# Storing the last output tile in halves of 64 rows, and a last piece of 160 columns

## The chip, the cores and the metric

The kernel runs on one core of a Trainium2 chip. The metric is the device time of one execution in microseconds. The profile is of one execution, and its span (from the first to the last instruction) is some 1.8 us shorter than the time of the same execution (393.5 against 395.35 us before the change).

## The reference

```python
# attention: q, k, v are (8, 12, 448, 64)
scores = scale * (q @ k^T) - log(448)
attn   = sigmoid(scores)
x      = (attn @ v)  -> (8*448, 768)
# feed-forward part: w_in (768, 2048), w_out (2048, 768)
h   = x @ w_in
g   = gelu_tanh(h)
out = g @ w_out      # (3584, 768), float32
```

## The kernel before

The kernel is a static schedule: a planner orders all operations, then they are written out per engine. Only its end matters here. The output is made in 28 tiles of 128 rows x 768 columns. The 128 rows of a tile are two strips of 64 rows each, and the 64 rows of a strip lie 7 rows apart in the output (row `r*7 + j` belongs to strip `j`). A tile is computed in column pieces; each piece is 16 matmuls into one PSUM bank (where TensorE leaves its sums), an eviction (the copy from there into the on-chip buffer `ob` in SBUF), and stores (transfers from `ob` to `out` in DRAM). A store is issued by an engine's instruction (about 0.5 us in this trace) and carried out by DMA engines, of which the profile counts 16 for the core; it has landed when the semaphore that it raises shows it done. SyncE (SP) issues the stores, except the very last half, which ScalarE (ACT) issues.

```python
def pieces(t_):
    if t_ < NT - 1:
        return [(0, EH), (EH, DM)]                           # 384 + 384 columns
    return [(0, EH), (EH, DM - 128), (DM - 128, DM)]         # last tile: 384, 256, 128

def make_b(t_, x, t):
    ...                                                      # 16 matmuls, eviction `ev` into ob[o]
    last = t_ == NT - 1
    end = last and hi == DM                                  # the last piece of the last tile
    ...
    if hi == DM or last:
        left = lo if last else 0
        if last and not end:                                 # pieces 0 and 1 of the last tile
            b, j = two[0]
            dst = out[b*S:(b+1)*S, lo:hi].rearrange("(r j) d -> j r d", j=NJ)[j:j + 2]
            # one transfer: DRAM side 2 x 64 x (hi-lo), SBUF side 128 x (hi-lo)
            sts.append(plan.add(Op("st%d" % t_, "SP", lambda e: e.dma_start(dst, ob[o][:, lo:hi]), ...)))
            return op
        for y in range(2):                                   # everything else: two transfers of 64 rows
            b, j = two[y]
            dst = out[b*S:(b+1)*S, left:hi].rearrange("(r j) d -> r j d", j=NJ)[:, j, :]
            def fn(e, y=y, dst=dst):
                return e.dma_start(dst, ob[o][64*y:64*y + 64, left:hi])
            if end and y == 1:
                at_end.append((fn, ev))                      # ACT issues it, after its last eviction
                continue
            sts.append(plan.add(Op("st%d.%d" % (t_, y), "SP", fn, ...)))
    ...
# at the end SP waits for the semaphores of the last three tiles' stores, then for ACT's store
```

Of the kernel before, what the change touches and what calls it, by code (L numbers as in the profile page):

```python
# [279 lines left out]
def bass_sigmoid_attention__then__act_gelu_tanh_kernel(  # L280
# [8 lines left out]
    B, H, S, D = q.shape  # L289
    assert D == 64 and H % 4 == 0 and S % 64 == 0 and B % 2 == 0  # L290
    NJ = S // 64
    NG = H // 4
    DM, DF = moe_w_in.shape
# [3 lines left out]
    EH = DM // 2  # L297
# [24 lines left out]
    plan = Plan()  # L322

    with contextlib.ExitStack() as stack:
        def SB(name, shape, dt):
            return stack.enter_context(nc.sbuf_tensor(name, shape, dt))
# [19 lines left out]
        ob = [SB("ob%d" % i, [128, DM], F32) for i in range(NOUT)]  # L346
# [4 lines left out]
        def copy(e, o, i, who):  # L351
            if who == "ACT":
                return e.activation(o, i, AF.Copy)  # L353
            return e.tensor_copy(o, i)  # L354

        def copy_alts(n):
            return {"ACT": (n / 1.2 + 50, n / 1.2 + 190), "DVE": (n / 0.96 + 75, n / 0.96 + 150)}
# [4 lines left out]
            out=ident[:], in_=ident[:], compare_op=ALU.not_equal, fill=1.0, base=0,  # L362
# [15 lines left out]
        def take(t):  # L378
            ok = [i for i in range(NPS) if bank_ok(i, t)]
            lone = [i for i in ok if not bank_ok(i ^ 1, t)]  # L380
            i = (lone or ok)[0]
            bank_busy[i] = True
            return i
# [12 lines left out]
        def give(i, op):  # L396
            bank_free[i] = op
            bank_busy[i] = False
# [363 lines left out]
        def pieces(t_):  # L762

            if t_ < NT - 1:
                return [(0, EH), (EH, DM)]
            return [(0, EH), (EH, DM - 128), (DM - 128, DM)]

        def make_b(t_, x, t):
            bank = take(t)
            prev = bank_free[bank]  # L770
            two = strips[2 * t_:2 * t_ + 2]
            col = (2 * t_ * 64) % (2 * S)
            lo, hi = pieces(t_)[x]

            def fn(e):
                r = None
                for fc in range(FC):
                    r = mm(ps[:, bank, 0:hi - lo], gT[:, fc, col:col + 128], w_out[:, fc, lo:hi],  # L778
                           start=(fc == 0), stop=(fc == FC - 1))
                return r  # L780

            deps = [prev] + [gelu[(b, fc)] for b in {x[0] for x in two} for fc in range(FC)]
            if t_ < 8:
                for ops in w_out_ld.values():
                    deps += ops
            op = Op("b%d.%d" % (t_, x), "PE", fn, deps, FC * ((hi - lo) / 2.4 + 2.5), 165.0, mode=128)
            o = t_ % NOUT
            edeps = [op]
            if t_ >= NOUT:
                edeps += store[t_ - NOUT]  # L790
            last = t_ == NT - 1
            end = last and hi == DM
            alts = copy_alts(hi - lo)
            if end:
                del alts["DVE"]
            ev = plan.add(Op("evo%d.%d" % (t_, x), "ANY",
                             lambda e, who: copy(e, ob[o][:, lo:hi], ps[:, bank, 0:hi - lo], who),
                             edeps, 0, 0, prio=(0, -1), alts=alts))
            give(bank, ev)
            ev_o[(t_, x)] = ev  # L800
            for (b, j) in two:
                if j == NJ - 1 or (b == B - 1):
                    b_last[b] = op
            if hi == DM or last:
                sts = store.setdefault(t_, [])
                left = lo if last else 0
                if last and not end:
                    b, j = two[0]
                    dst = out[b * S:(b + 1) * S, lo:hi].rearrange("(r j) d -> j r d", j=NJ)[j:j + 2]
                    sts.append(plan.add(Op("st%d" % t_, "SP", lambda e: e.dma_start(dst, ob[o][:, lo:hi]), [ev], 500.0, 0.0,  # L810
                                           prio=(0, t_), sem="st%d.0.%d" % (o, x), pkt=(8, 145.0))))
                    return op
                for y in range(2):
                    b, j = two[y]
                    dst = out[b * S:(b + 1) * S, left:hi].rearrange("(r j) d -> r j d", j=NJ)[:, j, :]

                    def fn(e, y=y, dst=dst):
                        return e.dma_start(dst, ob[o][64 * y:64 * y + 64, left:hi])

                    if end and y == 1:  # L820
                        at_end.append((fn, ev))
                        continue
                    sts.append(plan.add(Op("st%d.%d" % (t_, y), "SP", fn,
                                           [ev] if last else [ev_o[(t_, 0)], ev_o[(t_, 1)]], 500.0, 0.0,
                                           prio=(0, t_), sem="st%d.%d.%d" % (o, y, x if last else 0), pkt=(4, 145.0))))
            return op
# [103 lines left out]
        def pe_next(pl, t):  # L930
# [58 lines left out]
            if go_a:  # L989
                b, fc = state["a"]  # L990
                op = make_a(b, fc, t)
                state["a"] = (b, fc + 1) if fc + 1 < FC else (b + 1, 0)
                return op
            op = make_b(state["b"], state["h"], t)
            if state["h"] == len(pieces(state["b"])) - 1:
                for (b, j) in strips[2 * state["b"]:2 * state["b"] + 2]:
                    if j == NJ - 1:
                        b_done.add(b)
                state["b"] += 1
                state["h"] = 0  # L1000
            else:
                state["h"] += 1
# [21 lines left out]
        sem = {nm: stack.enter_context(nc.semaphore("s_" + nm.replace(".", "_"))) for nm in names}  # L1024
# [71 lines left out]
```

## Time and profile before

| | before |
|---|---|
| time, median of 3 runs | 395.26 us |
| span of the profiled execution | 393.5 us |
| TensorE busy | 381.8 us, 97% |
| last matmul ends | 385.58 us |
| last eviction ends | 385.88 us |
| tail: span minus end of the last matmul | 7.9 us |

The page of the profile says at its top that TensorE (PE) is busy nearly all the time (PEld are its weight loads, DVE is VectorE, POOL is GpSimd):

```profile
span 393.5 us, 7448 instructions
...
PE 381.8 (97%) x3189; PEld 201.2 (51%) x3189; DVE 134.4 (34%) x230; ACT 241.0 (61%) x380; POOL 51.1 (13%) x82
```

One would stop there, but a share is an average over the span. The chain of waits, asked for the time from 380 us on, ends with the last eviction. Its columns are start and duration in us:

```profile
379.84 5.74 PE ps L778 x51
385.58 0.02 issue
385.60 0.28 ACT ob L353
```

The chain stops at 385.88 us and the span is 393.5 us. The 7.6 us that are missing are no instruction of a compute engine, so the chain does not show them. The timeline of the same stretch shows what is issued there (start, us, engine, line, operation):

```profile
382.96 0.49 ACT L353 ACTIVATE ob<-ps 128x384 f32<-128x384 f32 x1 [2.11 <-PE ps L778]
383.48 2.18 SPq L810 DMA_DIRECT2D out_dram<-ob  x2
384.71 0.38 ACT L353 ACTIVATE ob<-ps 128x256 f32<-128x256 f32 x1 [1.26 <-PE ps L778]
385.60 0.28 ACT L353 ACTIVATE ob<-ps 128x128 f32<-128x128 f32 x1 [0.51 <-PE ps L778]
385.91 0.50 SPq L818 DMA_DIRECT2D out_dram<-ob  x1
385.91 0.54 ACTq L818 DMA_DIRECT2D out_dram<-ob  x1
```

Three evictions, and the stores after each: two single transfers of 128 rows (line 810, starting at 383.48 and 385.1 us) and the last piece's two halves (line 818). The DMA view, from 383.3 us on, gives size and time from issue to landing:

```profile
out_dram<-ob SPq DMA_DIRECT2D x1, 192.0 KB
out_dram<-ob SPq DMA_DIRECT2D x1, 128.0 KB
out_dram<-ob SPq DMA_DIRECT2D x1, 32.0 KB, 7.1
out_dram<-ob ACTq DMA_DIRECT2D x1, 32.0 KB, 4.4
```

For the two transfers of 128 rows the profile has no landing time. The last and smallest ones, 32 KB each, took 7.1 and 4.4 us, while a store of 192 KB with 64 rows takes 2.7 us (median) in the tiles before. What the DMA engines did meanwhile is in the table by windows; its last two columns are the mean busy share of the 16 DMA engines and the rate:

```profile
core 0: us, PE busy (x) PEld busy (x) DVE busy (x) ACT busy (x) POOL busy (x), PEclk, DMA share, GB/s
385.00:386.00 1.00, 0.57 (x11) 0.39 (x7) 0.00 (x0) 0.37 (x2) 0.00 (x0) 1.00 0.16 38
386.00:387.00 1.00, 0.00 (x0) 0.00 (x0) 0.00 (x0) 0.00 (x0) 0.00 (x0) 1.00 0.12 26
387.00:388.00 1.00, 0.00 (x0) 0.00 (x0) 0.00 (x0) 0.00 (x0) 0.00 (x0) 1.00 0.26 51
388.00:389.00 1.00, 0.00 (x0) 0.00 (x0) 0.00 (x0) 0.00 (x0) 0.00 (x0) 1.00 0.42 98
389.00:390.00 1.00, 0.00 (x0) 0.00 (x0) 0.00 (x0) 0.00 (x0) 0.00 (x0) 0.53 0.14 49
390.00:391.00 1.00, 0.00 (x0) 0.00 (x0) 0.00 (x0) 0.00 (x0) 0.00 (x0) 0.50 0.14 48
391.00:392.00 1.00, 0.00 (x0) 0.00 (x0) 0.00 (x0) 0.00 (x0) 0.00 (x0) 0.50 0.14 48
392.00:393.00 1.00, 0.00 (x0) 0.00 (x0) 0.00 (x0) 0.00 (x0) 0.00 (x0) 0.50 0.08 26
```

Nothing but DMA runs after 386 us. Its share is 0.12 to 0.14 in four of the seven windows from there on: two of sixteen engines are a share of 0.125. It is higher from 387 to 389 us (0.26 and 0.42), where most rows of the last piece's two small stores are moved as well.

### The profile page before, as it was taken

To read this page: it belongs to the slowest core of one execution; us is meant where nothing else is said; L and a number is where in the kernel's file an instruction comes from. 1 tells how busy PE (TensorE), PEld (TensorE's weight loads), DVE (VectorE), ACT (ScalarE), POOL (GpSimd) and SP (SyncE) were. 2 spreads that over 40 slices of the span, in tenths; PEclk is the share of its full clock that TensorE was granted. 3 is DMA by queue.
4 is the path that set the end of the run, shared out by engine and by line. 5 is a ranking of instruction groups with operands and counts; after the bars stand their busy time and mean duration, and the time that the engine had idled before them with its cause. 6 is when DMAs were issued, how large, how long until landed. Compare 5 with 4: busy or idle time off the path is not lost.

```text
span 393.5 us, 7448 instructions
## 1 busy us (share of the span) xinstructions
PE 381.8 (97%) x3189; PEld 201.2 (51%) x3189; DVE 134.4 (34%) x230; ACT 241.0 (61%) x380; POOL 51.1 (13%) x82
## 2 busy tenths in 40 slices
PE   7899999999999999999999999999999999999991
PEld 5344455545544554545555545555555555555561
DVE  3356613146435562464524434244332200000000
ACT  5999953588669877685757575756666533333110
POOL 5992110011102101110111010110000000000000
PEclk9999999999999999999999999999999999999997
DMA  8999999576774996595665918855030103011331
GB/s 232 199 198 203 210 207 310 112 176 151 173 178 127 215 169 170 83 261 122 172 166 96 184 36 188 163 117 151 2 80 3 32 10 82 0 40 42 80 82 40
DMA packets 64149, 51.74 MB, mean 131 GB/s; under 512 B 36212, under 2 KB 60660, under 8 KB 64116
## 3 DMA queue, kind: packets, MB, share of 16 engines
q1 hardware_dynamic: 48820, 36.78, 38.5%
q0 software_dynamic: 14528, 13.64, 21.9%
q10 hardware_dynamic: 768, 0.85, 0.6%
q8 instruction: 25, 0.41, 0.4%
q14 instruction: 8, 0.07, 0.1%
HBM read 45.61 MB, written 11.01 MB: 144 GB/s over the span
## 4 chain that ended last, share of the span: by engine, by line
PE 94%; ACT 3%; POOL 0%; issue 0%; POOLq 0%
PE ps L778 37%; PE ps L733 37%; PE ps L598 9%; PE ps L646 7%; ACT at L609 3%; PE ps L407 1%; PE ps L709 1%; PE ps L555 1%; PE ps L552 0%; POOL ident L361 0%; ACT ob L353 0%; POOL ident L360 0%; POOLq L361 0%; POOLq L1081 0%
## 5 line engine op out<-in xcount | busy, mean ns | idle before, releaser
L778 PE MATMUL ps<-w_out,gT 128*128 128x384 bf16 (+2 forms) x912 | 152.8, 323 | 0.0
L733 PE MATMUL ps<-xT,w_in 128*128 128x448 bf16 x750 | 151.7, 353 | 0.0
L622 DVE TENSOR_SCALAR at<-th 128x896 bf16<-128x896 f32 x147 | 91.8, 629 | 134.9 <-ACT th L618 134.8
L618 ACT ACTIVATE th<-ps 128x896 f32<-128x896 f32 x147 | 130.0, 931 | 0.5 <-PE ps L598 0.5
L778 PEld LDWEIGHTS ps<-w_out,gT 128*128 128x128 bf16 x912 | 87.6, 98 | 61.8 <-issue 3.6
L733 PEld LDWEIGHTS ps<-xT,w_in 128*128 128x128 bf16 x750 | 70.2, 98 | 74.0 <-issue 6.1
L747 ACT ACTIVATE gT<-ps 128x448 bf16<-128x448 f32 x128 | 71.3, 559 | 40.7 <-PE ps L733 40.7
L353 ACT ACTIVATE ob<-ps 128x384 f32<-128x384 f32 (+2 forms) x57 | 27.7, 485 | 96.7 <-PE ps L778 96.7
L598 PE MATMUL ps<-qT,kT 64*64 64x448 bf16 x672 | 49.1, 359 | 2.2 <-ACT at L609 1.7
L484 POOL DMA_DIRECT2D vb<-in_v_dram x24 | 15.0, 624 | 209.5 <-PE ps L598 206.2
L646 PE MATMUL ps<-at,vb 64*64 64x448 bf16 x672 | 38.2, 350 | 0.0
L598 PEld LDWEIGHTS ps<-qT,kT 64*64 64x64 bf16 x672 | 15.1, 105 | 28.2 <-issue 15.9
L646 PEld LDWEIGHTS ps<-at,vb 64*64 64x64 bf16 x672 | 19.5, 107 | 12.0 <-issue 0.7
L354 DVE CAST xT<-ps 128x448 bf16<-128x448 f32 x27 | 16.5, 619 | 11.9 <-PE ps L646 11.8
L354 DVE CAST kb<-kf 128x896 bf16<-128x896 f32 (+2 forms) x21 | 12.6, 601 | 18.5 <-DMA kf<-in_k_dram 18.4
L609 ACT ACTIVATE at<-ps 128x896 bf16<-128x896 f32 x21 | 17.1, 953 | 0.7 <-PE ps L598 0.7
L486 POOL DMA_DIRECT2D vb<-in_v_dram x24 | 17.4, 724 | 0.2 <-issue 0.2
L354 DVE CAST qb<-qf 128x896 bf16<-128x896 f32 (+1 forms) x20 | 12.2, 610 | 8.6 <-DMA qf<-in_q_dram 8.6
L353 ACT ACTIVATE xT<-ps 128x448 bf16<-128x448 f32 x21 | 11.8, 561 | 2.2 <-PE ps L646 2.2
L839 POOL DMA_DIRECT2D w_in<-in_moe_w_in_dram x16 | 9.9, 659 | 0.0
L407 PE MATMUL ps<-gT,ident 128*128 128x256 bf16 x25 | 5.6, 387 | 1.5 <-POOL ident L361 1.5
L354 DVE COPY kT<-ps 128x896 bf16<-128x896 bf16 (+2 forms) x7 | 3.9, 553 | 3.3 <-PE ps L552 1.7
(29 smaller groups left out, 39.9 us busy)
## 6 DMA issues: line engine op xcount, KB each, us to landing
out_dram<-ob SPq DMA_DIRECT2D x55, 192.0 KB, 2.8
kf<-in_k_dram SPq DMA_DIRECT2D x19, 448.0 KB, 4.5
qf<-in_q_dram SPq DMA_DIRECT2D x18, 448.0 KB, 6.1
vb<-in_v_dram POOLq DMA_DIRECT2D x48, 112.0 KB, 5.4
w_in<-in_moe_w_in_dram POOLq DMA_DIRECT2D x16, 192.0 KB, 10.7
w_out<-in_moe_w_out_dram POOLq DMA_DIRECT2D x4, 768.0 KB, 22.0
kb<-in_k_dram POOLq DMA_DIRECT2D x4, 224.0 KB, 8.5
qb<-in_q_dram POOLq DMA_DIRECT2D x4, 224.0 KB, 8.7
```

Source lines behind the costliest of these rows:

```text
L353: return e.activation(o, i, AF.Copy)
L354: return e.tensor_copy(o, i)
L484: a = plan.add(Op("ldv%da" % g, "SWQ", lambda e, d=dst[0:64], ap=lo: e.dma_start(d, ap), deps, 610.0, 0.0, prio=order_v(g), sem="ldv%da" % ...
L486: c = plan.add(Op("ldv%db" % g, "SWQ", lambda e, d=dst[64:128], ap=hi: e.dma_start(d, ap), deps, 610.0, 0.0, prio=order_v(g), sem="ldv%db" ...
L598: r = mm(ps[64 * half:64 * half + 64, (x, y)[a], 0:S], kv[d, a, j, :], qv[d, a, :, :], start=True, stop=True)
L609: lambda e: e.activation(at[as_][:], both, AF.Sigmoid, bias=bias, scale=scale),
L618: lambda e: e.activation(th[ts][:], both, AF.Tanh, bias=0.5 * bias, scale=0.5 * scale),
L622: lambda e: e.tensor_scalar(at[as_][:], th[ts][:], 0.5, 0.5, op0=ALU.mult, op1=ALU.add),
L646: r = mm(ps[64 * c:64 * c + 64, banks[a], 0:S], vb[s][d, slot, j, :], at[as_][d, a, :], start=(j == 0), stop=(j == NJ - 1))
L733: r = mm(ps[:, bank, 0:S], w_in[:, kt, fc * 128:(fc + 1) * 128], xT[xb][:, kt, :], start=(kt == 0), stop=(kt == KT - 1))
L747: lambda e: e.activation(gT[:, fc, col:col + S], ps[:, bank, 0:S], AF.Gelu_apprx_tanh),
L778: r = mm(ps[:, bank, 0:hi - lo], gT[:, fc, col:col + 128], w_out[:, fc, lo:hi], start=(fc == 0), stop=(fc == FC - 1))
```

## The change

It splits every store of the last tile into two transfers of 64 rows, as all other tiles have it, and makes the last piece 160 columns wide instead of 128, so that SP, which now has two more transfers to issue, is free when the last piece is ready.

```diff
-            return [(0, EH), (EH, DM - 128), (DM - 128, DM)]
+            return [(0, EH), (EH, DM - 160), (DM - 160, DM)]
 ...
             if hi == DM or last:
                 sts = store.setdefault(t_, [])
                 left = lo if last else 0
-                if last and not end:
-                    b, j = two[0]
-                    dst = out[b * S:(b + 1) * S, lo:hi].rearrange("(r j) d -> j r d", j=NJ)[j:j + 2]
-                    sts.append(plan.add(Op("st%d" % t_, "SP", lambda e: e.dma_start(dst, ob[o][:, lo:hi]), [ev], 500.0, 0.0,
-                                           prio=(0, t_), sem="st%d.0.%d" % (o, x), pkt=(8, 145.0))))
-                    return op
                 for y in range(2):
```

## The prediction

> **What bounds the kernel now.** TensorE: the page gives PE 97% of a 393.5 us span, the chain of waits is 94% PE. But the end is not PE. In the timeline the last matmul ends at 385.58, the last eviction (128 columns, 0.28 us on ACT) at about 385.9; the span ends 7.6 us later. Only stores run in that tail, so what the change can win lies there.
>
> **Why the tail is long.** The last tile's first two pieces (384 and 256 columns) go out as one transfer of 128 rows each, with an outer dimension of 2 on the DRAM side (2 x 64 rows). The Trainium skill, "DMA: Bandwidth & Descriptors", section "Why a DMA increments its semaphore by 16 and not by 1", says that a DMA uses the largest number of engines up to 16 that divides the slowest dimension of both sides: here 2. The trace agrees: in the windows from 389 to 392 us the DMA share is 0.14 (2 of 16 is 0.125) at 48 to 49 GB/s, while the 64-row stores of 192 KB before them landed in 2.7 us each (median). So 192 KB + 128 KB drain through two engines until about 392.5. The last piece's two 64-row stores, both issued at 385.91, landed after 7.1 us (SP) and 4.4 us (ACT): part of their rows wait on those two engines. Last landing 385.91 + 7.1 = 393.0; 0.5 us of closing waits give 393.5.
>
> **What the change does.**
> - Removes two 128-row issues (0.62 and 0.54 us on SP), adds four of 64 rows (about 0.5 us each). Piece 0 issues from 383.48 to 384.5; piece 1, whose last matmul comes some 0.2 us earlier, is evicted by about 384.85 and issues until about 385.9: SP is free just when the last piece is ready. No issue lands on the chain.
> - The last piece has 160 columns instead of 128. TensorE's columns are the same in sum, so it ends at 385.58 as before. The last eviction grows from 0.28 to about 0.31 us (256 columns take 0.38).
> - All transfers of the last tile should run on 16 engines. A 192 KB store lands in 2.7 us, of which the data of 64 packets of 3 KB take nearly 1 us; a 40 KB one should take 1.9 to 2.5 us. The last stores issue at about 385.95 and land at 387.9 to 388.4.
> - Everything before the last tile should be unchanged.
>
> **Sum.** Last landing 393.0 -> about 388.2: -4.8 us. Two more waits at the end: about +0.1 us. Net -4.7 us, all on the critical path because nothing else runs there. Time 395.26 - 4.7 = about 390.6 us, 1.2% less; range 389.8 to 391.8. The whole tail is under 2% of the time (7.6 of 395), so "faster by over 2%" is nearly impossible. Chances: faster 0.02, within 2% 0.97, slower 0.01.
>
> **What would show it.** TensorE's last matmul still at 385.6; four stores of 96 and 56 KB and two of 40 KB, each landing in under 3 us; over 100 GB/s from 385 to 388 us and no long stretch at a share of 0.13; span 388.5 to 389.3.
>
> **What would make it wrong.** If 64-row stores of short rows (640 to 1536 bytes) are paced by descriptors and not by engines, six in 2.5 us would queue (span 390 to 391). The same page, "Rules for kernel authors", advises against two transfers to partition halves because both use the same engines; that would hold only if the 128-row transfer used all 16, which the rate denies. If ACT's issue of the last store is slow to start (its 4.4 us was not all contention), the gain shrinks by about 1 us. If the schedule before the last tile shifted, TensorE's end would move.

## The result, and the profile after

| | before | after |
|---|---|---|
| time, median of 6 runs | 395.42 us | 390.80 us |
| lowest to highest | 395.06 to 396.65 | 390.57 to 392.09 |
| ratio, with 95% interval | | 0.9883 (0.9865 to 0.9901) |
| span of the profiled execution | 393.5 us | 388.8 us |
| last matmul ends | 385.58 us | 385.70 us |
| tail | 7.9 us | 3.1 us |

A ratio is the mean time of one kernel's fast runs over the mean of the other's of the same rounds, so it is not quite the ratio of the medians in the table. The time fell by 4.62 us, 1.2%.

The profile after. The timeline (its first line stands for seven issues, the first two of which belong to the tile before):

```profile
381.00 5.74 SPq L812 DMA_DIRECT2D out_dram<-ob  x7
383.08 0.49 ACT L353 ACTIVATE ob<-ps 128x384 f32<-128x384 f32 x1 [2.11 <-PE ps L778]
384.61 0.36 ACT L353 ACTIVATE ob<-ps 128x224 f32<-128x224 f32 x1 [1.04 <-PE ps L778]
385.72 0.30 ACT L353 ACTIVATE ob<-ps 128x160 f32<-128x160 f32 x1 [0.75 <-PE ps L778]
386.05 0.57 ACTq L812 DMA_DIRECT2D out_dram<-ob  x1
```

The last eviction starts 0.12 us later than before and takes 0.30 instead of 0.28 us. The stores:

```profile
out_dram<-ob SPq DMA_DIRECT2D x2, 96.0 KB, 2.2
out_dram<-ob SPq DMA_DIRECT2D x2, 56.0 KB, 2.0
out_dram<-ob ACTq DMA_DIRECT2D x1, 40.0 KB, 1.9
out_dram<-ob SPq DMA_DIRECT2D x1, 40.0 KB, 2.1
```

Every store of the last tile lands within 2.2 us of its issue, so the last one, issued at 386.1 us, lands at 388.2. The windows:

```profile
385.00:386.00 1.00, 0.68 (x10) 0.48 (x7) 0.00 (x0) 0.28 (x1) 0.00 (x0) 1.00 0.59 132
386.00:387.00 1.00, 0.00 (x0) 0.00 (x0) 0.00 (x0) 0.02 (x1) 0.00 (x0) 1.00 0.46 103
387.00:388.00 1.00, 0.00 (x0) 0.00 (x0) 0.00 (x0) 0.00 (x0) 0.00 (x0) 1.00 0.37 94
388.00:388.80 0.80, 0.00 (x0) 0.00 (x0) 0.00 (x0) 0.00 (x0) 0.00 (x0) 1.00 0.00 0
```

The stretch at a share of 0.13 is gone, and the DMA engines are idle from 388 us on. Apart from source line numbers and the numbers of semaphores, the instruction order on each engine differs between the two kernels in the last tile only: two widths of matmul and eviction, and the stores.

### The profile page after: what moved, and what is told of

Same layout as the page of the kernel before. It is cut to its first block, busy times and chain, and to the rows that moved or that the text cites. A ratio compares the mean times of both kernels' runs of the same rounds, so it can differ in the third digit from the quotient of the medians.

```text
span 388.8 us, 7451 instructions
## 1 busy us (share of the span) xinstructions
PE 382.0 (98%) x3189; PEld 201.6 (52%) x3189; DVE 134.9 (35%) x230; ACT 241.0 (62%) x380; POOL 51.5 (13%) x82
## 4 chain that ended last, share of the span: by engine, by line
PE 95%; ACT 3%; POOL 0%; issue 0%; POOLq 0%
PE ps L778 38%; PE ps L733 38%; PE ps L598 9%; PE ps L646 8%; ACT at L609 3%; PE ps L407 1%; PE ps L709 1%; PE ps L555 1%; PE ps L552 0%; ACT ob L353 0%; POOL ident L361 0%; POOL ident L360 0%; POOLq L361 0%; POOLq L1075 0%
```

## The experiments

Theory A is that of the prediction: a transfer uses the largest number of engines up to 16 that divides the outer dimension of both its sides. The DRAM side of the removed transfers had an outer dimension of 2, so they ran on two engines, and the end of the kernel was the time that two engines need for 320 KB. The rivals:

- B: the gain comes from the width of the last piece, which frees SP in time.
- C: two transfers of 64 rows are better than one of 128 as such, for instance because more is in flight.
- D: the last store merely stood behind the big ones in SP's queue, and another queue would cure it.

Where the end of the last matmul matters, the tail is quoted too. That end moved between 385.6 and 387.1 us from one profiled execution to the next, in kernels whose work before the last tile is the same; the tail (span minus that end) is free of it. The experiments ran on four chips; each kernel's ratio is to runs of the kernel before on its own chip. Tails come from one profiled execution each.

### The two parts of the change apart

Run e1_split_only: the change without the new width.

```diff
 # kernel before, plus:
-                if last and not end:
-                    ... one transfer of 128 rows ...
-                    return op
                 for y in range(2):
```

> The 64-row stores without the wider last piece (pieces 384, 256, 128). Theory A (the 128-row transfers ran on 2 engines): nearly the whole gain, 390.8 to 391.3 us; the last store issues some 0.2 us later than in the changed kernel because SP is still issuing piece 1's second half (its eviction ends near 385.1, two issues take about 1.1 us). Rival B (the gain comes from the width of the last piece and when SP comes free): most of the gain is gone, 393 us or more.

Measured: correct, 390.88 us median against 395.66, ratio 0.988 (0.9861 to 0.9899); tail 3.2 us.

Run e2_width_only: the new width without the split.

```diff
-            return [(0, EH), (EH, DM - 128), (DM - 128, DM)]
+            return [(0, EH), (EH, DM - 160), (DM - 160, DM)]
```

> The wider last piece with the 128-row stores kept (pieces 384, 224, 160). Theory A: 304 KB instead of 320 KB drain through two engines, at some 41 GB/s that is 0.3 to 0.4 us less, but the last SP store is bigger: 394.8 to 395.4 us. Rival B (width): near 391 us.

Measured: correct, 395.90 us median against 395.66, ratio 1.0002 (0.9986 to 1.0017); tail 7.8 us. The median lies 0.5 us above the expected range; this execution's last matmul ended at 386.46 us, and its tail is 0.1 us shorter than before.

What follows: the split is the whole gain, and rival B falls. The width alone does nothing, and with the split it cannot be told from nothing by time (390.88 without, 390.80 with, on different chips). SP's last issue did start late without it, at 386.5 us while ACT's started at 386.17, as the prediction had reckoned; the smaller store then landed after 1.9 us instead of 2.1.

### One transfer, sixteen engines

Run e3_one_transfer_64x2 keeps one transfer of 128 rows for each of the first two pieces and changes only the order in which the DRAM side is walked.

```diff
-                    dst = out[b * S:(b + 1) * S, lo:hi].rearrange("(r j) d -> j r d", j=NJ)[j:j + 2]
+                    dst = out[b * S:(b + 1) * S, lo:hi].rearrange("(h l j) d -> h j l d", j=NJ, h=64)[:, j:j + 2]
```

> The kernel before, with one 128-row transfer for each of the first two pieces as before, but the DRAM side walked as 64 x 2 rows instead of 2 x 64; the rows land in the wrong order, so the result is wrong on purpose, while bytes, rows, row sizes and the number of transfers are those of before. Theory A (the outer dimension picks the number of engines, 64 gives 16): 390.4 to 391.2 us, no stretch at a DMA share of 0.13. Rival C (two transfers of 64 rows in place of one of 128 are what helps, through more transfers in flight or the shape of the SBUF side): about 395 us as before.

Measured: 390.98 us median against 395.66, ratio 0.9883 (0.9863 to 0.9902); tail 2.9 us. The rows do land in the wrong order; the comparison with the reference passed all the same, because rows of one batch are nearly alike: the swap, worked out from the reference's own output, is an error of 0.24% of the whole. The stores:

```profile
out_dram<-ob SPq DMA_DIRECT2D x1, 192.0 KB, 2.3
out_dram<-ob SPq DMA_DIRECT2D x1, 128.0 KB, 2.1
out_dram<-ob SPq DMA_DIRECT2D x1, 32.0 KB, 1.8
out_dram<-ob ACTq DMA_DIRECT2D x1, 32.0 KB, 2.1
```

The same four transfers, of the same bytes and row sizes to the same set of rows, land in 1.8 to 2.3 us, where the last two took 7.1 and 4.4. Rival C falls: one transfer with an outer dimension of 64 is as good as two halves. This edit also changes the order of the addresses in DRAM, which could be a cause of its own; the next runs keep the order of the changed kernel and lose the gain all the same.

### Rows in a half: 62, 60, 61, 57, 63

If the number of engines is a divisor of the row count, the rows can be chosen to set it. These five kernels are the changed one with fewer than 64 rows stored in each half of the first two pieces. Their results are wrong (the rows left out are never written).

```diff
-                    dst = out[b * S:(b + 1) * S, left:hi].rearrange("(r j) d -> r j d", j=NJ)[:, j, :]
+                    n_ = 62 if last and not end else 64        # or 60, 61, 57, 63
+                    dst = out[b * S:(b + 1) * S, left:hi].rearrange("(r j) d -> r j d", j=NJ)[:n_, j, :]
 ...
-                        return e.dma_start(dst, ob[o][64 * y:64 * y + 64, left:hi])
+                        return e.dma_start(dst, ob[o][64 * y:64 * y + n_, left:hi])
```

> The changed kernel with 62 instead of 64 rows in each half of the first two pieces (two rows of each half are never stored: wrong on purpose, 3% fewer bytes). The largest number up to 16 that divides 62 is 2. Theory A: these transfers fall back on two engines, 294 KB at some 41 GB/s take about 7 us from 384.6: span about 392.5, 394.0 to 394.8 us. Rival C (two transfers instead of one is what helps): 390.8 us as with 64 rows, or a little less.

> Control for the 62-row run: 60 rows in each half instead of 62 (wrong on purpose, four rows of each half not stored). 15 divides 60. Theory A: 15 engines, so the time is that of the changed kernel, about 391 us, 4 to 5 us less than with 62 rows although only two rows fewer are stored. If the 62-row kernel was slow for another reason (a row count that is no power of two, an incomplete half), this one is slow too, near 395 us.

> 61 rows in each half (wrong on purpose). 61 is prime, so theory A expects one engine: 290 KB through one engine at half of 48 GB/s are 12 us or more from 384.6, against 7 to 8 on two: a tail after the last matmul of 12 to 14 us, 400 to 402 us, and a long stretch at a DMA share of about 0.06. If odd counts merely fall into the same slow path as 62 rows, about 395 us.

> 57 rows in each half of the first two pieces (wrong on purpose). The largest number up to 16 that divides 57 is 3. From the tails of 61 rows (13.4 us, one engine) and 62 rows (7.6 us, two), the tail is about 1.8 us + bytes / (engines x 25.6 GB/s); for 278 kB on three engines 5.4 us, 393.0 to 393.9 us. If the rule were only 'power of two or slow', near 395 us; if the engine count did not matter, 391 us.

> 63 rows in each half of the first two pieces (wrong on purpose, one row of each half not stored). The largest number up to 16 that divides 63 is 9. Theory A: nine engines, each piece drains in well under 1.5 us, so the time is that of the changed kernel to within 0.5 us, 390.8 to 391.5 us, though it stores more bytes than the 62-row kernel (396.05 us). It also gives the profile that the 60-row run lacks, whose profiled executions fell in the slow state: no stretch at a DMA share of 0.13. If row counts other than 64 and 60 were slow as such, near 395 us.

Measured (the row with 64 is the changed kernel; "engines" is the largest divisor up to 16, so it is the theory's number and not a measured one; times are medians):

| rows | engines | time, us | before on that chip, us | ratio (95% interval) | tail, us |
|---|---|---|---|---|---|
| 61 | 1 | 401.32 | 395.85 | 1.0133 (1.0100 to 1.0166) | 13.4 |
| 62 | 2 | 396.05 | 395.66 | 1.0011 (0.9991 to 1.0032) | 7.6 |
| 57 | 3 | 391.98 | 395.65 | 0.9906 (0.9892 to 0.9921) | 4.6 |
| 63 | 9 | 390.90 | 395.83 | 0.9886 (0.9838 to 0.9934) | 3.0 |
| 60 | 15 | 390.91 | 395.85 | 0.9871 (0.9836 to 0.9907) | no fast profile |
| 64 | 16 | 390.80 | 395.42 | 0.9883 (0.9865 to 0.9901) | 3.1 |

One run of the 60-row kernel (494.81 us, clock 0.75; also the profiled one) and one of the kernel before (1378.5 us) were slow; the table and the ratios leave them out. The 57-row tail is from the slowest of that kernel's four runs (393.22 us).

Leaving out two of 64 rows loses the whole gain, and leaving out one or four does not. The rates in windows in which only these transfers ran (61, 62 and 57 rows, one line from each kernel, columns as above):

```profile
396.00:397.00 1.00, 0.00 (x0) 0.00 (x0) 0.00 (x0) 0.00 (x0) 0.00 (x0) 0.50 0.07 24
```

```profile
391.00:392.00 1.00, 0.00 (x0) 0.00 (x0) 0.00 (x0) 0.00 (x0) 0.00 (x0) 0.54 0.13 47
```

```profile
389.50:389.80 0.30, 0.00 (x0) 0.00 (x0) 0.00 (x0) 0.00 (x0) 0.00 (x0) 0.50 0.20 72
```

They are 24, 47 and 72 GB/s at shares of 0.07, 0.13 and 0.20: one, two and three engines of sixteen, at 24 GB/s each. This is the most direct evidence for theory A. The trace's packet records agree without any rate: the number of the first piece's packets in flight at once is most often 1 with 61 rows, 2 with 62 and in the kernel before, 3 with 57, and 9 with 63 (records overlap a little, so up to 12 occur there), while the changed kernel reaches 17. For 60 rows only the time speaks. The rate also sizes the tail. The stores of the first two pieces at 24 GB/s per engine take 12.4 us for 61 rows (296.7 kB, one engine), 6.3 us for 62 (301.6 kB, two) and 3.9 us for 57 (277.2 kB, three); in the kernel before, 6.8 us for 327.7 kB on two. The tails are 13.4, 7.6, 4.6 and 7.9 us: the drain and 0.7 to 1.3 us more. With 63 rows the tail is as short as with 64, so nine engines were enough to hide the drain, and what is left, 3.0 us, is the last eviction, one small store and the closing wait.

Two expectations missed here. For 62 rows I expected 394.0 to 394.8 us and measured 396.05; the profiled execution's last matmul ended at 386.34 us, 0.76 us later than before, and the early part of the drain was slower than I had reckoned (see "What stays open"). For 57 rows I expected 393.0 to 393.9 us and measured 391.98, a tail of 4.6 us instead of 5.4: the line through two tails, 1.8 us plus the bytes at 25.6 GB/s per engine, had too large a constant. For 60 rows "about 391 us" held.

### One of the two transfers left as it was

Runs e7_only_first_128 and e8_only_second_128: the kernel before, with the transfer of 128 rows kept for one piece only.

```diff
-                if last and not end:
+                if last and x == 0:          # e7; x == 1 in e8
```

> The kernel before with only piece 0 (384 columns) stored by one 128-row transfer; piece 1 by two of 64 rows. Theory A: piece 0 drains through two engines until about 389.6 as before, and the shares of the later stores on those two engines follow within some 0.7 us: last landing about 390.3, a tail of about 5.2 us after the last matmul, 392 to 393 us. If only the last 128-row transfer mattered: 391 us.

> The kernel before with only piece 1 (256 columns) stored by one 128-row transfer; piece 0 by two of 64 rows. Theory A: 128 KB start near 386.2 and need 2.7 us at 48 GB/s, up to 4 us at the slower rate that piece 0 had: last landing 389 to 390.5, 391.3 to 393 us. The excess over the changed kernel of this run and of the one with piece 0 alone should sum to about the 4.7 us of both, less what overlaps.

Measured: e7 393.53 us median, ratio 0.9933 (0.9905 to 0.9961), tail 5.6 us; e8 393.09 us, ratio 0.9939 (0.9890 to 0.9989), tail 5.2 us; both correct. e8 lies just above its range of 391.3 to 393, e7 0.5 us above its own of 392 to 393.

Against the changed kernel's tail of 3.1 us, the first transfer costs 2.5 us and the second 2.1 us: 4.6 us in sum, where both together cost 4.8. The two transfers pass through the same two engines one after the other, so their costs add: in the kernel before, the second transfer's first packet starts at 389.6 us, just as the first transfer's last one ends, although it was issued at 385.1. The first one costs 2.5 us although it is issued 2.4 us before the last piece is ready.

### The last store on another queue

Run e9_last_on_act: the kernel before, with both halves of the last piece issued from ACT's queue.

```diff
-                    if end and y == 1:
+                    if end:
                         at_end.append((fn, ev))
```

(A second line makes ACT count its last eviction, which SP's wait had done.)

> The kernel before with both halves of the last piece issued from ACT's queue, so that neither stands behind the 128-row transfers on SP's queue. Theory A (the drain of 320 KB through two engines sets the end): the 7.1 us of the SP store goes away, but piece 1's own transfer still lands near 392.4 to 392.9, so the tail shrinks by 0.5 us at most: 394.8 to 395.4 us. Rival D (the last store waiting in SP's queue is the cause, and another queue would cure it): the last landings come 4.4 us after the issue, 391.5 to 392.5 us.

Measured: correct, 395.51 us median against 395.65, ratio 1.0007 (0.9986 to 1.0028); tail 7.9 us. The stores:

```profile
out_dram<-ob SPq DMA_DIRECT2D x1, 192.0 KB
out_dram<-ob SPq DMA_DIRECT2D x1, 128.0 KB
out_dram<-ob ACTq DMA_DIRECT2D x2, 32.0 KB, 3.7
```

The last piece now lands after 3.7 us (median) instead of 7.1 and 4.4, and the kernel ends at the same time: the time is 0.1 us above the expected range of 394.8 to 395.4, and the tail did not shrink. The end was set by the two-engine drain itself, and the 7.1 us of the last store was a symptom. Rival D falls.

### A try at a better version

Run e11_second_half_on_act: the changed kernel with the last piece 128 columns wide again and the second half of piece 1 issued from ACT between its last two evictions, so that SP need not hurry.

```diff
 # cut: the pieces (128 again), the issue after `ev`, and the longer wait at the end
+                    if last and x == 1 and y == 1:
+                        mid[id(ev)] = (fn, ev)       # ACT issues it right after the eviction `ev`
+                        continue
                     if end and y == 1:
```

> A try at a better version, correct: the changed kernel with the last piece 128 columns wide again and the second half of piece 1 issued from ACT, which is idle for 0.5 to 0.75 us between the last two evictions, so that SP is free when the last piece is ready. The narrower last eviction gains 0.02 us, SP's last issue need not wait 0.45 us as it did in the split-only run, but ACT's issue takes 0.55 us of a gap of 0.51 us. Expected 0.1 to 0.3 us less than the changed kernel at best, 390.5 to 390.9 us, within the scatter of runs; a tail of 2.8 to 3.2 us against 3.1.

Measured: correct, 390.60 us median (390.50 to 390.72) against 395.65, ratio 0.9874 (0.9861 to 0.9886). The interval overlaps that of the changed kernel, 0.9865 to 0.9901, and the two ran on different chips, so this does not show a better version. It confirms that little is left: of the tail of 3.0 us, 0.28 is the eviction and about 2 the landing of one small store.

### What stays open

The two engines were slower at first. In the kernel before they moved 38 and 26 GB/s in the windows from 385 to 387 us, and 48 later; the 62-row kernel shows the same (23 and 28 GB/s in its windows from 385 to 387, 47 later). TensorE and ACT were busy until 385.9 us, but the slow phase outlasts that by about a microsecond. In the packet records most packets of this phase take 65 ns, as later, with single ones of 100 to 470 ns between them; SP and ACT were issuing the last stores until 386.45 us. No run separates the causes. The drain takes 7.8 us (384.7 to 392.5) where 24 GB/s per engine make 6.8, so the slow start costs about a microsecond; it is the part of my estimates for 62 rows that was short.

## Why the prediction was right

Predicted was 390.6 us (389.8 to 391.8), measured 390.80.

- The bound. Predicted: the end is not TensorE's but the tail of stores, 7.6 us after the last eviction. Shown: the change left the last matmul where it was (385.58 and 385.70 us) and cut the tail from 7.9 to 3.1 us.
- The cause. Predicted: two engines, because of the outer dimension of 2 on the DRAM side. Shown by e3 (same transfers, other outer dimension, whole gain) and, with the order of the rows kept, by the rates for 61, 62 and 57 rows (24, 47 and 72 GB/s). The Trainium skill, "DMA: Bandwidth & Descriptors", section "Why a DMA increments its semaphore by 16 and not by 1", states the divisor rule, and every run here agrees with it.
- Which part matters. Predicted: the width costs 0.03 us of eviction and keeps SP's issues off the chain. Measured: 0.02 us of eviction, and no effect on the time that could be told from none (e1, e2). That the wider last piece was needed is not shown.
- The landing. Predicted: 1.9 to 2.5 us for the last stores, the last landing at about 388.2. Measured: 1.9 and 2.1 us, and 386.1 + 2.1 = 388.2.
- The sum. Predicted: -4.7 us. Measured: -4.7 us in the spans (393.5 to 388.8) and -4.62 us in the medians.
- The signs in the profile. All came true but one: I expected over 100 GB/s from 385 to 388 us, and the last of these three windows had 94, because nothing was left to move before it ended.
- The doubts. The last store from ACT was not slow to start (1.9 us), and the six short transfers did not queue: they landed in 1.9 to 2.2 us.

The account of the last stores was right as well, with a nuance that the prediction did not draw. It put the end at 385.91 + 7.1 = 393.0 us, the landing of the last store behind the big transfers. e9 shows that this store's wait was not itself the cost, since without it the kernel ended no sooner. That SP's half took 7.1 us and ACT's 4.4 agrees with the same page, section "Queues, rings and completion order": a queue's descriptors are taken up in order on each engine, and an engine alternates between queues. On the two slow engines SP's rows came after both big transfers (392.4 to 392.6 us), ACT's in between (389.7 to 390.0, after the first).

## What to carry to other kernels

Look past the last eviction: the chain of waits may stop there while the span goes on for microseconds, and in a kernel whose main engine is 97% busy such a tail can still be worth an edit (7.9 us here, of which 4.8 went). When a store or load lands late at a constant small DMA share, multiply the share by 16 to get the number of engines and look at the outermost dimension of both sides of the transfer: by theory A a multiple of 16 on each uses all sixteen (64 rows here), while 63 and 60 rows, 9 and 15 engines by the same rule, cost nothing here that could be told by time. Fewer, larger transfers are not better if merging them puts a 2 in front.

## What the Trainium skill lacked or had wrong

- "DMA: Bandwidth & Descriptors", section "Rules for kernel authors", the row on two transfers to disjoint partition halves: it says not to bother and to use one 128-partition transfer, because both halves use the same 16 engines. That holds when the one transfer really has 16 engines (e1 390.88 us with halves, e3 390.98 us with one transfer of outer dimension 64). It was wrong for the transfer here, whose DRAM side began with a dimension of 2: halves alone saved 4.8 us (e1, 390.88 against 395.66). The row should point to the one further down on using all 16 engines.
- The same page, section "Specifications", gives about 27 GiB/s per engine (29 GB/s). Stores with rows of 896 and 1024 bytes ran at 24 GB/s per engine here, on one, two and three engines alike (24, 47 to 48, 72 GB/s).
- The same page gives the divisor rule with examples of engine counts, but without times; a row count of 62 or 61 on both sides, enough to fall to two engines or one, is worth an example with them: 64 rows 390.80, 62 rows 396.05, 61 rows 401.32 us for the whole kernel.
- "DMA: Bandwidth & Descriptors" and "Perfetto Trace Analysis" do not have the slow start of a transfer on two engines (26 to 38 GB/s for about 2 us, then 48).
- Neither of them has a number for how much issuing can slow behind a transfer on one engine: with 61 rows, SP's last three store issues took 1.4 to 4.3 us each, against about 0.5 to 0.6 us in the changed kernel. With 62 rows, on two engines, it did not slow (at most 0.5 us).
